# Filler matmuls dealt out anew, and a sum of 17 shared between two engines, in a fused attention and feed-forward kernel

## The chip, the cores and the metric

The kernel runs on one core of one Trainium2 chip. A core has TensorE (matmul; PE in the profile, with its weight loads in a row of their own, PEld), VectorE (DVE), ScalarE (ACT), GpSimd (POOL) and SyncE (SP, which here issues DMAs). Each engine works through its own queue in order, and waits on semaphores for others. TensorE writes to PSUM, eight banks of 512 float32 per partition; GpSimd doesn't reach PSUM. The metric is the time of one execution on the device in microseconds (us); lower is better.

## What is computed

The reference, cut to what matters (S = 2048 rows, D = 512, 32 heads of 16, F = 1792):

```python
def _A_ref(x, wqkv, wo):
    qkv = (x @ wqkv).reshape(B, S, 3, H, Dh).transpose(2, 0, 3, 1, 4)
    q, k, v = qkv[0], qkv[1], qkv[2]
    phi = lambda t: jnp.where(t > 0, t + 1, jnp.exp(t)) + 1e-6
    pq, pk = phi(q), phi(k)
    kv = jnp.einsum("bhsd,bhse->bhde", pk, v)
    z = jnp.einsum("bhsd->bhd", pk)
    num = jnp.einsum("bhqd,bhde->bhqe", pq, kv)
    den = jnp.einsum("bhqd,bhd->bhq", pq, z)[..., None] + 1e-6
    o = num / den
    return o.transpose(0, 2, 1, 3).reshape(B, S, D) @ wo

def _B_ref(x, w_gate, w_up, w_down):
    g = _silu(x @ w_gate)
    u = x @ w_up
    return (g * u) @ w_down

xn = _layernorm(x, axis=-1)
return x + _A_ref(xn, A_wqkv, A_wo) + _B_ref(xn, B_w_gate, B_w_up, B_w_down)
```

The change touches `den`: for each row and head, the sum of 16 products `pq * z` and of 1e-6.

## The kernel before

The 2048 rows are 16 tiles of 128. The kernel goes through four parts, and within each the Python code writes out the order of every engine's queue by calling small helpers; `K.add` records an operation with what it reads and writes, and the semaphore waits follow from that.

1. Up to about 48 us: layernorm, projections of keys and queries, the map phi, and the sums over all rows (key-value and z).
2. To about 68 us: gate and up projections for the first 384 rows (tiles 0 to 2), while weights are rescaled.
3. To about 153 us: gate and up for the other 1664 rows, in fourteen **steps**, one for each 128 columns of F (`for fc in range(NFC)`, L1135). Here a 2 x 2 block product is done with seven block products in place of eight (Strassen and Winograd's scheme). In each step every product is a pair of matmuls of 416 columns (`prod`, L869 to 884), for each of two groups of rows, q = 0 and 1: 28 matmuls.
4. To the end: the down projection of those rows by the same scheme with 256-column matmuls (`dprod`, L1079), six pairs of tiles, with the attention output of each tile added on top (`attn`, L1093, four matmuls). The seam between parts 3 and 4 is called **the passage** here: the end of step 13, `first(0)` (product 1 of the first pair of tiles), what fillers are left, and the first products behind them.

**A step's order.** TensorE: product 1 for q = 0, 1; product 5 for both; then products 2 and 6 of q = 0 and of q = 1; then filler units; then products 3 and 7 of q = 0 and of q = 1; filler units again; then product 4 of both. Between these, for each q:

- ScalarE copies product 1 negated into a second bank (`seed`, L891) and product 5 into SBUF (`keep5`, L896), and takes the silu of two finished banks (`gate0`, L906, and `gate1`, L911).
- VectorE takes the saved product 5 less the bank after product 6 and puts it where product 3 then accumulates (`u4`, L916): product 3 waits for it. After product 7 it saves a difference to `c22` (`up22`, L921), and only then may product 4 accumulate on that bank. After product 4 it multiplies with the silu (`h21`, L931).
- GpSimd multiplies `c22` with the silu (`h22`, L925).

**Beside this a step carries** for VectorE the sums of weight blocks for the next pair of steps (`w_sums`, L842: one operation in even steps, two in odd ones); for ScalarE a rescaling of weights (L834) and, in some steps, a sum of squares over a block of w_down (`square_d`, L782, not needed before step 6's end); and the division by `den` for one tile:

- GpSimd multiplies `pq` with z into `pz` (`pz_mul`, L657), two tiles ahead. `pz` has two buffers of 32 heads by 17 float32: 16 products, and the last place holds 1e-6, written once by ScalarE (`pz_floor`, L650).
- VectorE sums the 17 (`den_sum`, L663) at the end of the step before, and takes the reciprocal (`den_turn`, L669) in the step, between `u4` and `up22`.
- GpSimd multiplies `pq` with it (`pq_mul`, L676), at the end of the step's queue and made to wait for `w_sums`; then comes `pz_mul` of the tile two ahead. SyncE transposes the tile by DMA (`turn`, L682).

Steps 0 to 10 do this for tiles 0 to 10 (their slot numbers are the same); the other five tiles are done in part 4.

**Filler units.** `todo` (L935) holds 72 single matmuls of 512 columns, the down projection and attention of tiles 0 to 3 (`ounits`, L700 to 711: 18 units for each, into banks 0 and 1). `fill(n)` (L938) puts the next n of them on TensorE's queue. Three are put into step 0 at L1140; `FILLS` (L1133) has for each step how many go ahead of product 3 (L1163) and how many between product 7 and product 4 (L1170); what is left goes behind `first(0)` in the passage (L1222). With the 32nd and the 36th unit the results of tiles 0 and 1 are complete, and `oout` adds x on VectorE (L720) and stores the tile; then the banks are used for tiles 2 and 3.

**In the passage** ScalarE copies the last hidden block, rescaled, into the layout of part 4 (`hcopy`, L1061), then copies product 1 (`dseed`, L1101), for which the attention matmuls (L1095) on that bank wait. VectorE then forms sums of hidden blocks (`h_sum`, L1073) and of w_down blocks (`t_sum`, L1024; `t1_part`, L1015), saves one result (`dkeep_y`, L1109) and combines two banks (`du4`, L1115), for which product 7 waits.

Of the kernel before, what the change touches and what calls it, by code (L numbers as in the profile page):

```python
# [7 lines left out]
ALU = mybir.AluOpType  # L8
# [112 lines left out]
def bass_parallel_sum__linear_attn_block__swiglu_ffn__prompt_kernel(nc, A_x, A_wqkv, A_wo, B_x, B_w_gate, B_w_up, B_w_down, out):  # L121
    xin = A_x[0]
    oview = out[0]
    K = _Program()
    bf, f32 = dt.bfloat16, dt.float32

    with contextlib.ExitStack() as es:
        E = es.enter_context

        def sb(name, shape, dtype):  # L130
            return E(nc.sbuf_tensor(name, shape, dtype))
# [17 lines left out]
        pq = sb("pq", [P, NT, D], bf)  # L149
# [9 lines left out]
        zbc = sb("zbc", [P, D], f32)  # L159
        pz = sb("pz", [P, 2, NH * (DH + 1)], f32)  # L160
        den = sb("den", [P, 2, NH], f32)
# [45 lines left out]
        junks = [b_[:, :, :].rearrange("p a b -> p (a b)").bitcast(bf)[:, 0:F // 2] for b_ in (p5, c22)]  # L207
        xs = sb("xs", [P, 2, 2 * H7], f16)
        asd = sb("asd", [P, 8], f32)
# [61 lines left out]
        for t in range(4, 16):  # L271
# [5 lines left out]
            out=ident[:, :], in_=ident[:, :], compare_op=ALU.not_equal, fill=1.0,  # L277
# [362 lines left out]
        def heads(ap):  # L640
            return ap.rearrange("p (h d) -> p h d", d=DH)


        pzh = [pz[:, i, :].rearrange("p (h d) -> p h d", d=DH + 1) for i in (0, 1)]

        def pz_floor(t):
            i = SLOT[t] % 2
            last = pzh[i][:, :, DH:DH + 1].rearrange("p h d -> p (h d)")
            one = nc.const_aps.tensor(1.0, (P, NH), bf)
            K.add("act", lambda e: e.activation(last, one, ACT.Copy, scale=flo[:, t:t + 1] if t in CENTRED else 1e-6),  # L650
                  r=[("flo", t)] if t in CENTRED else [("den", i)], w=[("pz", i)])

        def pz_mul(t, after=()):
            if SLOT[t] < 4:
                pz_floor(t)
            i = SLOT[t] % 2
            K.add("pool", lambda e: e.tensor_tensor(  # L657
                out=pzh[i][:, :, 0:DH], in0=heads(pq[:, t, :]), in1=heads(zbc[:, :]), op=ALU.mult),
                  r=[("pq", t), ("zbc",)] + list(after), w=[("pz", i)])

        def den_sum(t):
            i = SLOT[t] % 2
            K.add("dve", lambda e: e.tensor_reduce(  # L663
                out=den[:, i, :], in_=pzh[i], axis=mybir.AxisListType.X, op=ALU.add),
                r=[("pz", i)], w=[("den", i)])

        def den_turn(t):
# [18 lines left out]
        def divide(t):  # L686
            den_sum(t)
            den_turn(t)
            pq_mul(t)
            turn(t)  # L690
            pz_mul(t + 2)
# [232 lines left out]
        def h22(q, fc):  # L924
            K.add("pool", lambda e: e.tensor_tensor(  # L925
                out=hj(fc)[:, TB + q * TS:TB + (q + 1) * TS], in0=c22[:, q, :], in1=sil4[:, 2 + q, :], op=ALU.mult),
                r=[("c22", q), ("sil4", 2 + q)], w=[("hj", fc, 2 + q)], a=hjold(fc))
# [10 lines left out]
        def fill(n):  # L938
            for _ in range(min(n, len(todo))):
                fn, r, w, after = todo.pop(0)  # L940
                K.add("pe", fn, r=r, w=w)
                busy[w[0]] = after is None
                if after is not None:
                    after()

        for t in (0, 2):
# [15 lines left out]
            "u": top_square, "g": gather, "T": lambda: total(1), "C": lambda: scales(1),  # L962
            "a": lambda k, p: scale(("wg", "wu")[k], p), "p": lambda k, p: scale(("wg", "wu")[k], p, "pool"),
            "X": x_sum, "W": lambda h: w_sums(0, h), "Z": z_total, "z": lambda i: pz_mul(ORDER[i]), "d": square_d,
            "G": lambda c, e: gt_evac(c, "act" if e else "dve"), "m": m_mm, "k": kv_mask,
            "h": gather_d, "D": total_d, "e": scales_d, "s": lambda i: smalls_d()[i]()}

        def prepare(text):
            for w in text.split():
                steps2[w[0]](*[int(v) for v in w[1:]])  # L970
# [7 lines left out]
        for j in range(NFC):  # L978
# [5 lines left out]
            prepare(BESIDE.get(j, ""))  # L984
        Wt = [w_[:, 2 * i:2 * i + 2, 0:2 * H7] for w_ in (wg, wu) for i in (0, 1)]
        wtk = [(key + "c", fc) for key in ("wg", "wu") for fc in range(7)]
# [4 lines left out]
        def split(ap):  # L991
            return ap.rearrange("p (s c) -> p s c", s=2)

        Tt = {2: Wt[0].bitcast(f16), 3: xs[:, :, :], 1: split(mixb[:, 0:4 * H7].bitcast(f16)),
              4: wg[:, 0:2, 2 * H7:].bitcast(f16)}

# [129 lines left out]
        def pz_ahead(t, after=()):  # L1126
            i = SLOT[t] + 2
            if i < NT:
                pz_mul(ORDER[i], after)

        SC = {1: [("wg", 2, "act")], 2: [("wu", 3, "act")], 3: [("wg", 3, "act")], 4: [("wu", 4, "act")], 5: [("wg", 4, "act")], 6: [("wu", 5, "act")], 7: [("wg", 5, "act")], 8: [("wg", 6, "act")], 9: [("wu", 6, "act")]}
        LATE = {10: [(11, 0)], 11: [(11, 1)]}
        FILLS = ((3, 4), (2, 3), (1, 3), (3, 5), (1, 4), (1, 2), (0, 2), (2, 2), (1, 3), (1, 3), (1, 3), (1, 2), (3, 3), (6, 1))  # L1133
        DIV = {i + 0: ORDER[i] for i in range(11)}
        for fc in range(NFC):  # L1135
            for q in (0, 1):
# [15 lines left out]
            p = fc // 2  # L1152
            if fc == 0 and 0 in DIV:
                den_sum(DIV[0])
# [7 lines left out]
            prepare(BESIDE.get(14 + 2 * fc, ""))  # L1162
            fill(FILLS[fc][0])  # L1163
            for q in (0, 1):
# [4 lines left out]
                h22(q, fc)  # L1169
            fill(FILLS[fc][1])  # L1170
            for q in (0, 1):
# [29 lines left out]
            if fc + 1 in DIV:  # L1201
                den_sum(DIV[fc + 1])
# [21 lines left out]
        for p in range(NP2 - 1):  # L1224
            a, b, d = GB[p % 2]
            t = DIV2.get(p)
# [60 lines left out]
        p = NP2 - 1  # L1287
# [58 lines left out]
```

## Time and profile before

| | |
|---|---|
| median of three runs | 200.21 us (200.05 to 200.54) |
| the profiled execution | 200.1 us |
| its span, first to last instruction | 198.9 us |
| granted TensorE clock over the span | 1.00 |
| HBM read, written | 9.70 MB, 2.10 MB |

A row of the profile gives the line of the kernel, the engine, the operation, what it writes and reads by the program's tensor names, the shapes, and how often (x). Times of a timeline row are the start in us from the span's beginning and the duration; in brackets stands how long the engine had been idle and which engine, tensor and line ended that. Neighbouring rows of one kind are merged (x2), and the duration then covers both. In the view of busy time by stretch, each row has the stretch, its length, and the busy time and instruction count of each engine. `pb` is PSUM. `h22` and others write into tensors that served earlier purposes (`hT`, `xn`, `pq`), so one line can show several names. The clock of TensorE was granted in full throughout, so a matmul of a kind takes the same time everywhere.

### The profile page before, as it was taken

Reading aid. Unit: us, or ns where it says so; the run is one execution under the profiler, and the core shown is the slowest. Engines: PE = TensorE matmul, PEld = TensorE weight load, DVE = VectorE, ACT = ScalarE, POOL = GpSimd, SP = SyncE. Lnnn points to the kernel's source line nnn. Section 1 sums busy time; section 2 is a strip of 40 time slices with the busy share of each in tenths; the row PEclk is TensorE's granted clock in tenths of the full one; section 3 lists DMA queues with packets and bytes.
Section 4 is the critical chain, followed back from the end, with each engine's and each line's share of the span. In section 5 each row is a group of like instructions: output and inputs, shape, how many; then the busy total and the mean of one; then the engine's idle time right before and its main releaser. Section 6 shows DMA issues by size and latency. Waiting matters only on the chain.

```text
span 198.9 us, 3554 instructions
## 1 busy us (share of the span) xinstructions
PE 194.7 (98%) x1193; PEld 114.5 (58%) x1207; DVE 172.1 (87%) x328; ACT 157.2 (79%) x314; POOL 124.0 (62%) x152
## 2 busy tenths in 40 slices
PE   8999999999999999999999999999999999999995
PEld 2344444444655545555554455555555788888884
DVE  3999999996997898886899998887987999998886
ACT  4799887699798997998988888998897968575300
POOL 3787877799999388667577667868678004413220
PEclk9999999999999999999999999999999999999999
DMA  6943457899900000111110211111000012132123
GB/s 173 357 130 81 58 107 218 229 289 373 313 4 0 3 0 0 28 30 26 28 40 13 56 26 26 26 26 31 2 0 2 3 40 66 30 79 66 44 67 120
DMA packets 28899, 15.97 MB, mean 80 GB/s; under 512 B 17232, under 2 KB 28880, under 8 KB 28880
## 3 DMA queue, kind: packets, MB, share of 16 engines
q1 hardware_dynamic: 28320, 15.28, 28.8%
q10 hardware_dynamic: 560, 0.46, 0.7%
q8 instruction: 9, 0.15, 0.3%
q14 instruction: 10, 0.08, 0.2%
HBM read 9.70 MB, written 2.10 MB: 59 GB/s over the span
## 4 chain that ended last, share of the span: by engine, by line
PE 94%; DVE 2%; DMA 1%; issue 1%; ACT 0%; POOL 0%; SPq 0%
PE pb L881 35%; PE pb L1089 16%; PE pb L443 13%; PE pb L564 9%; PE pb L492 7%; PE pb L704 5%; PE pb L1095 5%; PE pb L708 2%; DMA x_sb<-in_A_x_dram 1%; PE pb L624 0%; PE pb L696 0%; DVE pq L482 0%; PE pb L406 0%; POOL ef L471 0%; DVE stats L306 0%
## 5 line engine op out<-in xcount | busy, mean ns | idle before, releaser
L676 POOL TENSOR_TENSOR pq<-pq,rden 128x512 bf16<-128x512 bf16 x16 | 16.9, 1056 | 37.2 <-DVE rden L669 26.7
L881 PE MATMUL pb<-xnT,wgu 128*128 128x416 bf16 x112 | 26.6, 339 | 0.0
L443 PE MATMUL pb<-wqkv,xnT 128*128 128x512 bf16 x110 | 25.1, 380 | 0.2
L657 POOL TENSOR_TENSOR pz<-pq,zbc 128x512 f32<-128x512 bf16 x16 | 18.9, 1179 | 5.0 <-ACT pz L650 3.5
L911 ACT ACTIVATE zacc<-pb,iw 128x416 bf16<-128x416 f32 x28 | 16.6, 613 | 4.4 <-PE pb L881 3.5
L564 PE MATMUL pb<-xnT,wgu 128*128 128x384 bf16 x112 | 19.9, 326 | 0.1
L921 DVE TENSOR_TENSOR c<-pb,p 128x416 f32<-128x416 f32 x28 | 16.4, 589 | 3.9 <-PE pb L881 1.9
L925 POOL TENSOR_TENSOR hT<-c,zacc 128x416 bf16<-128x416 f32 x16 | 15.3, 976 | 6.7 <-DVE c L921 4.1
L471 POOL TENSOR_SCALAR ef<-ef 128x512 bf16<-128x512 bf16 x25 | 15.5, 620 | 5.8 <-ACT ef L464 5.6
L443 PEld LDWEIGHTS pb<-wqkv,xnT 128*128 128x128 bf16 x112 | 10.9, 98 | 13.4 <-DVE pk L482 0.4
L916 DVE TENSOR_TENSOR pb<-p,pb 128x416 f32<-128x416 f32 x28 | 16.3, 593 | 2.1 <-PE pb L881 0.8
L464 ACT ACTIVATE ef<-pb 128x512 bf16<-128x512 f32 x25 | 14.8, 593 | 3.9 <-PE pb L443 3.9
L509 POOL TENSOR_TENSOR zacc<-zacc,pk 128x512 f32<-128x512 f32 x13 | 16.0, 1232 | 1.0
L891 ACT ACTIVATE pb<-pb 128x416 f32<-128x416 f32 x28 | 13.4, 500 | 3.4 <-PE pb L881 2.4
L881 PEld LDWEIGHTS pb<-xnT,wgu 128*128 128x128 bf16 x112 | 10.9, 98 | 8.8 <-ACT pb L891 0.3
L906 ACT ACTIVATE zacc<-pb,iw 128x416 bf16<-128x416 f32 x28 | 15.7, 625 | 0.0
L564 PEld LDWEIGHTS pb<-xnT,wgu 128*128 128x128 bf16 x112 | 10.9, 98 | 7.0
L1089 PE MATMUL pb<-wgu,xnT 128*128 128x256 f16 (+1 forms) x112 | 14.9, 273 | 0.0
L881 PE MATMUL pb<-xnT,wqkv 128*128 128x416 bf16 x56 | 14.4, 340 | 0.2
L881 PE MATMUL pb<-GT,wqkv 128*128 128x416 f16 x56 | 14.4, 339 | 0.0
L881 PE MATMUL pb<-wo,wqkv 128*128 128x416 f16 x56 | 14.4, 339 | 0.0
L1095 PE MATMUL pb<-M,pk 128*128 128x256 bf16 x96 | 13.6, 273 | 0.0
(201 smaller groups left out, 489.3 us busy)
## 6 DMA issues: line engine op xcount, KB each, us to landing
x_sb<-in_A_x_dram SPq DMA_DIRECT2D x14, 128.0 KB, 4.1
wgu<-in_B_w_gate_dram SPq DMA_DIRECT2D x2, 896.0 KB, 5.5
wgu<-in_B_w_up_dram SPq DMA_DIRECT2D x2, 896.0 KB, 7.8
wd<-in_B_w_down_dram SPq DMA_DIRECT2D x2, 896.0 KB, 12.4
out_dram<-out_sb SPq DMA_DIRECT2D x24, 64.0 KB, 1.6
wqkv<-in_A_wqkv_dram SPq DMA_DIRECT2D x3, 256.0 KB, 4.7
wqkv<-in_A_wqkv_dram SPq DMA_DIRECT2D x1, 512.0 KB, 6.6
wo<-in_A_wo_dram SPq DMA_DIRECT2D x1, 512.0 KB, 8.3
```

Of the source, the lines that this page charges most:

```text
L443: K.add("pe", [(lambda e, c=c: e.matmul(banks[b][:, :], src[:, c, t * P:(t + 1) * P], wqkv[:, c, col:col + D], start=(c == 0), stop=(c == ...
L509: K.add("pool", lambda e: e.tensor_tensor(out=dst, in0=acc, in1=more, op=ALU.add), r=[key, mkey], w=[dkey])
L564: fns.append(lambda e, c=c, b=b, w_=w_: e.matmul(banks[b][:, 0:T0], w_[:, c, fc * P:(fc + 1) * P], xnT[:, c, 0:T0], start=(c == 0), stop=( ...
L657: K.add("pool", lambda e: e.tensor_tensor(out=pzh[i][:, :, 0:DH], in0=heads(pq[:, t, :]), in1=heads(zbc[:, :]), op=ALU.mult), r=[("pq", t) ...
L676: K.add("pool", lambda e: e.tensor_tensor(out=heads(pq[:, t, :]), in0=heads(pq[:, t, :]), in1=rden[:, i, :][:, :, None].broadcast_to([P, N ...
L881: K.add("pe", [(lambda e, c=c: e.matmul(banks[bank][:, 0:TS], L[i][:, c, :], R[i][:, c, ts], start=(start and c == 0), stop=(c == 1), skip ...
L906: K.add("act", lambda e: e.activation(sil4[:, q, :], bk(a), ACT.Silu, scale=iw[:, 0:1]), r=[B(a), ("iw",)], w=[("sil4", q)], a=[("zacc", 0 ...
L911: K.add("act", lambda e: e.activation(sil4[:, 2 + q, :], bk(d), ACT.Silu, scale=iw[:, 0:1]), r=[B(d), ("iw",)], w=[("sil4", 2 + q)], a=[(" ...
L916: K.add("dve", lambda e: e.tensor_tensor(out=bk(d), in0=p5[:, q, :], in1=bk(b), op=ALU.subtract), r=[B(b), ("p5", q)], w=[B(d)])
L921: K.add("dve", lambda e: e.tensor_tensor(out=c22[:, q, :], in0=bk(b), in1=p5[:, q, :], op=ALU.subtract), r=[B(b), ("p5", q)], w=[("c22", q)])
L1089: K.add("pe", [(lambda e, k=k: e.matmul(split(banks[b][:, 0:HD]), L[:, k, :], cut[:, :, k * P:(k + 1) * P], start=(start and k == 0), stop ...
L1095: K.add("pe", [(lambda e, g=g: e.matmul(dk(b), pk[:, SLOT[t], g * P:(g + 1) * P], M[:, g, lo:lo + HD], start=False, stop=(g == NG - 1), sk ...
```

## The change

It has two parts. `FILLS` gets other counts: in (ahead of product 3, ahead of product 4),

| step | 0 | 1 | 2 | 3 | 4 | 5 | 6 | 7 | 8 to 10 | 11 | 12 | 13 | passage |
|---|---|---|---|---|---|---|---|---|---|---|---|---|---|
| before | 3, 4 | 2, 3 | 1, 3 | 3, 5 | 1, 4 | 1, 2 | 0, 2 | 2, 2 | 1, 3 | 1, 2 | 3, 3 | 6, 1 | 3 |
| after | 3, 4 | 2, 3 | 1, 3 | 3, 3 | 1, 3 | 1, 3 | 1, 3 | 1, 3 | 1, 3 | 1, 2 | 2, 3 | 4, 2 | 5 |

Units keep their order. The 32nd falls in step 4 before and in step 5 after, the 36th in step 6 in both.

And `pz` is laid out anew: 8 products, 1e-6, 8 products for each head. `pz_mul` writes the two halves to their places, for all 16 tiles. For slots 3 to 8 GpSimd then adds the second half to the first (`fold`, 32 x 8 float32, in place), behind `pz_mul` on its queue, so in steps 1 to 6 of the program's order; and VectorE's sum of these six tiles, at the end of steps 2 to 7, reads 9 places per head in place of 17. On the other engines the instructions and their order stay, but for where the units stand and that `oout` of tile 0 moves with its unit.

```diff
+FOLD = range(3, 9)
...
+        def two(ap):
+            return ap.rearrange("p (h c d) -> p h c d", h=NH, c=2)
+
+        def halves(i):
+            v = pz[:, i, :]
+            return bass.AP(v.tensor, v.offset, [list(v.ap[0]), [DH + 1, NH], [DH // 2 + 1, 2], [1, DH // 2]])
+
         pzh = [pz[:, i, :].rearrange("p (h d) -> p h d", d=DH + 1) for i in (0, 1)]
 
         def pz_floor(t):
             i = SLOT[t] % 2
-            last = pzh[i][:, :, DH:DH + 1].rearrange("p h d -> p (h d)")
+            last = pzh[i][:, :, DH // 2:DH // 2 + 1].rearrange("p h d -> p (h d)")
...
             K.add("pool", lambda e: e.tensor_tensor(
-                out=pzh[i][:, :, 0:DH], in0=heads(pq[:, t, :]), in1=heads(zbc[:, :]), op=ALU.mult),
+                out=halves(i), in0=two(pq[:, t, :]), in1=two(zbc[:, :]), op=ALU.mult),
                   r=[("pq", t), ("zbc",)] + list(after), w=[("pz", i)])
+            if SLOT[t] in FOLD:
+                fold(t)
+
+        def fold(t):
+            i = SLOT[t] % 2
+            lo, hi = pzh[i][:, :, 0:DH // 2], pzh[i][:, :, DH // 2 + 1:]
+            K.add("pool", lambda e: e.tensor_tensor(out=lo, in0=lo, in1=hi, op=ALU.add), r=[("pz", i)], w=[("pz", i)])
 
         def den_sum(t):
             i = SLOT[t] % 2
             K.add("dve", lambda e: e.tensor_reduce(
-                out=den[:, i, :], in_=pzh[i], axis=mybir.AxisListType.X, op=ALU.add),
+                out=den[:, i, :], in_=pzh[i][:, :, 0:DH // 2 + 1] if SLOT[t] in FOLD else pzh[i], axis=mybir.AxisListType.X, op=ALU.add),
                 r=[("pz", i)], w=[("den", i)])
...
-        FILLS = ((3, 4), (2, 3), (1, 3), (3, 5), (1, 4), (1, 2), (0, 2), (2, 2), (1, 3), (1, 3), (1, 3), (1, 2), (3, 3), (6, 1))
+        FILLS = ((3, 4), (2, 3), (1, 3), (3, 3), (1, 3), (1, 3), (1, 3), (1, 3), (1, 3), (1, 3), (1, 3), (1, 2), (2, 3), (4, 2))
```

## The prediction

> **What bounds the kernel now.** First the page: the busy shares, and the chain that ended last by engine.
>
> ```profile
> PE 194.7 (98%) x1193; PEld 114.5 (58%) x1207; DVE 172.1 (87%) x328; ACT 157.2 (79%) x314; POOL 124.0 (62%) x152
> PE 94%; DVE 2%; DMA 1%; issue 1%; ACT 0%; POOL 0%; SPq 0%
> ```
>
> TensorE carries the chain from end to end, and the change keeps every one of its matmuls. So the time can fall only by what TensorE still waits, and rise only by new waits. How much it waits is read from the steps. In the view of busy time by stretch I cut steps 3 to 8 where each step's first matmul of product 1 starts. The columns are the stretch, its length, then the busy time of PE, weight loads, VectorE, ScalarE and GpSimd, then clock and DMA.
>
> ```profile
> 87.28:93.93 6.65, 6.65 (x38) 3.52 (x36) 5.01 (x10) 6.08 (x12) 4.83 (x6) 1.00 0.11 22
> 93.93:99.93 6.00, 5.95 (x33) 3.17 (x33) 5.41 (x11) 6.00 (x13) 3.54 (x5) 1.00 0.11 23
> 99.93:105.58 5.65, 5.65 (x33) 2.86 (x31) 5.18 (x11) 5.09 (x10) 4.06 (x5) 1.00 0.18 46
> 105.58:111.17 5.59, 5.54 (x30) 2.69 (x30) 5.30 (x11) 4.98 (x10) 4.09 (x5) 1.00 0.12 23
> 111.17:117.06 5.89, 5.89 (x34) 3.02 (x33) 5.46 (x15) 5.08 (x10) 4.09 (x5) 1.00 0.19 47
> 117.06:122.85 5.79, 5.74 (x33) 3.07 (x33) 5.03 (x11) 5.31 (x12) 4.23 (x5) 1.00 0.11 23
> ```
>
> Steps 3 to 8 hold 8, 5, 3, 2, 4 and 4 filler units. From 6.65 and 6.00 a unit costs (6.65 - 6.00) / 3 = 0.217 us, and the 28 matmuls of a step alone 4.92 (0.176 each); with 4 units that makes 5.79, which step 8 shows. Against 4.92 + 0.217 n, step 5 (5.57) loses 0.08, step 6 (5.35) 0.24, step 7 (5.79, and 0.03 for one small matmul) 0.07: 0.39 us. PE's busy column hides this, since the ends of matmuls are modelled. The weight loads show it, with what they waited for in brackets; step 6, then the passage:
>
> ```profile
> 107.87 0.27 PEld L881 LDWEIGHTS pb<-GT,wqkv 128*128 128x128 f16 x2
> 108.54 0.11 PEld L881 LDWEIGHTS pb<-xnT,wqkv 128*128 128x128 f16 x2 [0.40 <-DVE pb L916]
> ```
> ```profile
> 152.65 0.11 PEld L881 LDWEIGHTS pb<-wqkv,wgu 128*128 128x128 bf16 x2 [0.53 <-DVE c L921]
> ...
> 154.45 0.33 PEld L1095 LDWEIGHTS pb<-M,pk 128*128 128x128 bf16 x4 [0.36 <-ACT pb L1101]
> ...
> 158.57 0.66 PEld L1089 LDWEIGHTS pb<-xs,zacc 128*128 128x128 f16 x7 [0.29 <-DVE pb L1115]
> ```
>
> Not all of a load's idle time is lost. It holds the usual gap between loads and the load's lead over its own matmul, together about one matmul and the gap: 0.25 between 416-column matmuls (0.176 + 0.08, the gap left by 0.27 for two loads of 0.10), 0.33 behind a filler (0.217 + 0.12), 0.12 between the passage's 256-column ones (0.11 + 0.01). So of 0.40 in step 6 about 0.15 is lost, of 0.53 0.28, of 0.36 0.03 and of 0.29 0.17. So product 4 of step 13 loses 0.28 to VectorE's L921, the attention block 0.03, product 7 of the passage 0.17: 0.48. With the steps 0.87 us are within reach.
>
> **Why VectorE is late in steps 5 to 7.** Its queue from the end of step 5 into step 7:
>
> ```profile
> 105.35 1.09 DVE L931 TENSOR_TENSOR hT<-pb,zacc 128x416 bf16<-128x416 f32 x2 [0.19 <-PE pb L881]
> 106.36 0.42 DVE L842 TENSOR_TENSOR wqkv<-wqkv,wgu 128x512 f16<-128x512 f16 x1
> 106.81 0.42 DVE L842 TENSOR_TENSOR wqkv<-wgu,wqkv 128x512 f16<-128x512 bf16 x1
> 107.15 0.71 DVE L663 TENSOR_REDUCE den<-pz 128x32 f32<-128x544 f32 x1
> 107.89 1.30 DVE L916 TENSOR_TENSOR pb<-p,pb 128x416 f32<-128x416 f32 x2
> 109.10 0.34 DVE L669 RECIPROCAL rden<-den 128x32 f32<-128x32 f32 x1
> 109.46 1.29 DVE L921 TENSOR_TENSOR c<-pb,p 128x416 f32<-128x416 f32 x2
> 110.67 0.68 DVE L720 TENSOR_TENSOR out_sb<-pb,x_sb 128x512 bf16<-128x512 f32 x1
> 111.27 1.08 DVE L931 TENSOR_TENSOR hT<-pb,zacc 128x416 bf16<-128x416 f32 x2
> 112.26 0.68 DVE L842 TENSOR_TENSOR wqkv<-wgu 128x1024 f16<-128x1024 bf16 x1
> 112.86 0.15 DVE L787 TENSOR_REDUCE as<-asd 128x1 f32<-128x8 f32 x1
> 113.05 0.16 DVE L790 TENSOR_SCALAR as1b<-as 128x1 bf16<-128x1 f32 x1
> 113.12 0.71 DVE L663 TENSOR_REDUCE den<-pz 128x32 f32<-128x544 f32 x1
> 113.75 1.08 DVE L916 TENSOR_TENSOR pb<-p,pb 128x416 f32<-128x416 f32 x2
> ```
>
> From L916 to L916 it needs 5.86, in a step that TensorE could do in 5.35. Two things load it: the output row L720 (in steps 4 and 6, where units 32 and 36 end) and a step made short by few fillers.
>
> **The fillers.** Steps 3 to 7 now hold 6, 4, 4, 4 and 4 units, 22 as before, so TensorE's own work in them stays 29.4. Unit 32 and its L720 move to step 5; unit 36 stays in step 6. What does VectorE need in a step of 5.79? Take t = 0 at L916, which starts 2.31 into step 6: ten matmuls (1.76) and 0.55 for a pair to run through. Product 4's first pair is then done at 24 x 0.176 + 4 x 0.217 + 0.55 = 5.64, t = 3.33. There L931 starts; L842 is done at 5.0 in even steps and 5.2 in odd ones, den (0.71) at 5.64 and 5.83, and the next L916 is due at 5.79. L720 fits the gap between L921 (done by 2.95) and L931 and pushes that by only 0.11; the two small operations of step 6 add 0.34. Fillers alone would leave L916 late by some 0.15 in step 6 and 0.25 in step 7.
>
> **The shorter sum** takes that away. den reads 288 values in place of 544. From L663 (0.71 for 544) and L787 (0.15 for 8) a value costs 1.05 ns, so 0.44: 0.27 less, six times (0.34 less if it halved; nothing if its 32 rows set the price). At 0.44 den is done at 5.67 in step 5 and 5.77 in step 6, in time for 5.79. The 0.39 goes, unless ScalarE is late.
>
> **ScalarE, which the new deal uncovers.** In the table steps 3 and 4 keep it busy 6.08 + 6.00 = 12.08 us; they shrink from 12.65 to 6.22 + 5.79 = 12.01.
>
> ```profile
> 93.54 0.94 ACT L782 ACTIVATE xs<-wd 128x896 bf16<-128x896 bf16 x1
> 94.38 0.19 ACT L782 ACTIVATION_READ_ACCUMULATOR xs<-wd 128x1 f32 x1
> 94.48 0.98 ACT L891 ACTIVATE pb<-pb 128x416 f32<-128x416 f32 x2
> 95.37 0.92 ACT L896 ACTIVATE p<-pb 128x416 f32<-128x416 f32 x2
> ```
>
> L782 is a sum of squares with no reader nearby, but L891 and L896 stand behind it, and L916 waits for the first L896, done at about 95.89 (a pair takes 0.92 with some overlap). Two units fewer bring step 4 to 93.50, its L916 due at 93.50 + 2.31 = 95.81; L896 holds it to 95.92. The single filler ahead of product 3 hides L916 almost exactly, so step 4 loses 0.1 (0 to 0.25). Step 5 has ScalarE busy for 5.09 only and recovers. Net for steps 3 to 7: 0.39 - 0.10 = 0.29.
>
> **Steps 12, 13 and the passage.** One unit leaves each step and both go behind product 1 of the passage, so TensorE comes to step 13's products 3 and 4 one and up to two units (0.43) earlier, and has five units to fill the passage.
>
> ```profile
> 151.30 1.29 DVE L921 TENSOR_TENSOR c<-pb,p 128x416 f32<-128x416 f32 x2 [0.59 <-PE pb L881]
> 152.57 1.24 DVE L931 TENSOR_TENSOR pq<-pb,zacc 128x416 bf16<-128x416 f32 x2
> 154.16 0.63 DVE L1073 TENSOR_TENSOR xn<-wqkv,xn 128x896 f16<-128x896 bf16 x1 [0.36 <-ACT xn L1061]
> ```
>
> L921 idles 0.59 for product 7, so it can come 0.59 earlier, while product 4 comes 0.43 earlier: its wait falls from 0.28 to 0.12. L916 of step 13 has less cover; I put 0.06 on that. The attention block's 0.03 goes. That is 0.28 - 0.12 - 0.06 + 0.03 = 0.13. Then L931, ScalarE's copy L1061 and L1073 follow in a chain that starts at product 4's first pair, 0.43 - 0.06 = 0.37 earlier. VectorE has no idle from L1073 to near L1115, so that comes 0.37 earlier, TensorE 0.13: product 7's 0.17 goes too. Sum 0.30 (0.10 to 0.45).
>
> **What GpSimd pays.**
>
> ```profile
> 110.13 1.91 POOL L925 TENSOR_TENSOR hT<-c,zacc 128x416 bf16<-128x416 f32 x2 [0.64 <-DVE c L921]
> 113.02 1.06 POOL L676 TENSOR_TENSOR pq<-pq,rden 128x512 bf16<-128x512 bf16 x1 [0.98 <-DVE as L787]
> 114.04 1.16 POOL L657 TENSOR_TENSOR pz<-pq,zbc 128x512 f32<-128x512 bf16 x1
> ```
>
> No row has the fold (256 values, float32). From L657 (512 in 1.16) and L925 (416 in 0.96) a value costs 2.1 ns and an instruction 0.09: 0.63, and some 0.08 to wait for the product it adds. Its bounds are 0.58 (half of L657) and 0.96 (L925). Behind it on the queue stands L925, which idles 0.64 there: it comes 0.1 later, and only the next step's L921 waits for its buffer. L657 now writes runs of 8 for all 16 tiles: between 1.06 (L676) and twice its price, 2.3; I take 1.16, as the runs of 16 that it writes now cost 2.3 ns a value, what L925's whole rows cost. The Trainium skill speaks against the fold: "GPSIMD Engine Reference", section 4.1, gives elementwise work to VectorE because GpSimd is about 2x slower at it. By that rule 0.63 buys 0.27 here, which matters only if GpSimd is on the path (rival b); the page has it 62% busy.
>
> **Sum.** 0.29 + 0.30 = 0.59, less 0.03 for a den later than I count it: 0.56. The profiled run took 200.1 (a span of 198.9 and 1.2 around it) and the median of three runs is 200.21: 199.54 on the one, 199.65 on the other. I forecast 199.6.
>
> **Rivals.**
> (a) *The waits only change place*: 200.1. For it: one filler hides L916 with almost nothing to spare in every step, ScalarE is late in step 4, den may cost by rows. Steps 3 to 7 then gain 0.1 and the passage 0.05. Against it: step 8 waits for nothing with the same 4 units and a den of 0.71.
> (b) *GpSimd becomes the loop, slower than before*. L676 waits for L842; L657, the fold and two L925 follow it; and L842 is held up when it meets L925:
>
> ```profile
> 147.14 1.38 DVE L1024 TENSOR_TENSOR wgu<-wgu,mixb 128x896 f16<-128x896 bf16 x1
> ```
>
> An operation of this size took 0.63 with GpSimd idle (L1073 above); here 1.38, beside L925. The loop is 0.08 + 2.18 for L676 and L657 + 0.71 + 1.91 + 0.55 to 0.85 for L842: 5.4 to 5.7, against 5.79. It decides once L657 and the fold take over 2.0 together and not 1.8. At 2.3 + 0.63 it is 0.9 over in each of six steps, 5.6 us in all; a tenth of that excess already eats the gain. A middling case, 2.3 together (1.4 and 0.9): 0.3 x 6 - 0.56 = 1.2 slower, 201.4; at 2.17, 200.7. The Trainium skill, "SBUF — State Buffer", section "Who interferes with whom", has it that a VectorE operation with two SBUF inputs and a GpSimd one that reads SBUF block each other entirely; the 1.38 agrees.
> (c) *All 0.87 goes*, step 4's wait too: 199.3.
>
> **Chances.** Forecast 0.48, (a) 0.25, (b) 0.15, (c) 0.12. About 0.3% (0.6 us) is what a measurement of this kernel can tell from no change. The forecast's 0.56 lies next to that line: of its 0.48 I give 0.24 to faster and 0.24 to within. Faster: 0.24 + 0.12 + 0.02 of (a) = 0.38. Slower: 0.15 + 0.03 of (a), should step 4 lose its whole 0.25 and more = 0.18. Within: 0.44. The range is 199.2 to 200.8, from just past (c) to the milder half of (b); the forecast's own, by its bounds, 199.3 to 200.0.
>
> **What would show it.** Right: steps 4 to 7 at 5.79 to 5.9 each, no load idle of 0.40 at product 3 of step 6, den at 0.44, a fold of about 0.63 done before VectorE's first L921 ends, no wait at product 7 of the passage; in step 4 L916 starting with ScalarE's L896. Wrong: L657 over 1.3, L842 stretched beside L925 in steps 2 to 7, steps over 5.9, or a den that stays near 0.7.

## The result, and the profile after

| | before | after |
|---|---|---|
| median | 200.24 us (13 runs, 200.05 to 201.43) | 199.59 us (13 runs, 199.34 to 200.25) |
| span of the profiled execution | 198.9 us | 198.3 us |

The ratio is 0.9959, with a 95% interval of 0.9945 to 0.9972: about 0.4% faster. In the changed kernel line numbers are higher, by 15 behind the fold: u4 is L931 (L916 before), up22 L936 (L921), h21 L946 (L931), h22 L940 (L925), seed L906 (L891), keep5 L911 (L896), pz_mul L665, the fold L674, den_sum L678, pq_mul L691, w_sums L857, the sum of squares L797, a step's matmuls L896. The page after, busy shares and chain:

```profile
PE 194.6 (98%) x1193; PEld 115.8 (58%) x1207; DVE 171.1 (86%) x328; ACT 157.2 (79%) x314; POOL 128.3 (65%) x158
PE 97%; DVE 1%; issue 0%; POOL 0%; ACT 0%
```

TensorE still carries the chain, with 97% in place of 94%; VectorE's 2% are 1% now. Where the time went is seen in the view of busy time by stretch, cut where each part's first weight load starts: steps 0 to 2, 3 to 7, 8 to 12, and step 13 to the end. Before, then after:

```profile
68.12:87.10 18.98, 18.88 (x102) 9.92 (x103) 16.57 (x29) 17.37 (x37) 13.91 (x13) 1.00 0.07 14
87.10:116.89 29.79, 29.69 (x163) 15.26 (x164) 26.32 (x54) 27.24 (x51) 20.62 (x21) 1.00 0.14 32
116.89:146.11 29.22, 29.06 (x159) 15.42 (x161) 24.63 (x46) 26.27 (x53) 21.86 (x22) 1.00 0.09 19
146.11:198.86 52.75, 50.46 (x429) 41.12 (x428) 46.23 (x88) 29.55 (x43) 14.83 (x15) 1.00 0.18 49
```
```profile
68.29:87.28 18.99, 18.89 (x103) 9.94 (x104) 16.56 (x29) 17.38 (x37) 14.60 (x14) 1.00 0.07 14
87.28:116.80 29.52, 29.41 (x162) 15.66 (x163) 25.37 (x53) 27.21 (x51) 23.95 (x27) 1.00 0.14 32
116.80:145.81 29.01, 28.85 (x158) 15.34 (x160) 24.40 (x46) 26.22 (x53) 21.56 (x22) 1.00 0.09 19
145.81:198.33 52.52, 50.36 (x430) 41.45 (x429) 46.15 (x88) 29.60 (x43) 15.40 (x15) 1.00 0.19 49
```

The first column is the one to read. Steps 3 to 7 give 0.26 (the ends of the stretches are rounded), step 8 to the end 0.21 + 0.23 = 0.44 (of the 0.21, almost all is one filler that moved behind step 13). From step 0 on that is 130.74 - 130.04 = 0.70. The part before step 0, in which only the places of `pz` that are written differ, ends at 68.12 in the one profile and at 68.29 in the other, and takes back 0.17. Such shifts come with every profile (68.12 to 68.75 over all those of this study), so below kernels are compared from step 0 on. There, a part without a change repeats to within 0.03.

The steps 3 to 8 after:

```profile
87.45:93.67 6.22, 6.22 (x36) 3.32 (x34) 4.75 (x10) 5.65 (x11) 5.08 (x7) 1.00 0.12 24
93.67:99.59 5.92, 5.87 (x32) 2.99 (x32) 4.83 (x11) 5.92 (x14) 4.21 (x5) 1.00 0.11 24
99.59:105.38 5.79, 5.79 (x34) 3.07 (x33) 5.37 (x11) 5.51 (x10) 5.08 (x7) 1.00 0.11 23
105.38:111.16 5.78, 5.73 (x32) 3.07 (x32) 5.33 (x13) 5.06 (x10) 4.69 (x6) 1.00 0.18 45
111.16:116.98 5.82, 5.82 (x35) 3.22 (x34) 5.10 (x15) 5.08 (x10) 4.90 (x6) 1.00 0.20 48
116.98:122.77 5.79, 5.74 (x33) 3.08 (x33) 4.84 (x11) 5.24 (x12) 4.13 (x5) 1.00 0.11 23
```

Steps 5, 6 and 7 take what TensorE's own work takes (5.79, and 0.03 more in step 7); step 4 loses 0.13. The weight loads of step 4 (product 2 of q = 0) and of the passage:

```profile
95.20 0.11 PEld L896 LDWEIGHTS pb<-xnT,wgu 128*128 128x128 bf16 x2 [0.37 <-ACT pb L906]
```
```profile
151.91 0.11 PEld L896 LDWEIGHTS pb<-wqkv,wgu 128*128 128x128 bf16 x2 [0.31 <-DVE c L936]
...
153.93 0.51 PEld L1110 LDWEIGHTS pb<-M,pk 128*128 128x128 bf16 x4
...
158.06 0.66 PEld L1104 LDWEIGHTS pb<-xs,zacc 128*128 128x128 f16 x7
```

Product 4 of step 13 waits less (0.31 idle against 0.53, and the load ahead of it doesn't wait any more), the attention matmuls and product 7 not at all. The view of waits adds up what the steps' loads waited for up22. Before, then after:

```profile
PEld pb L881 <- DVE c L921: 2.0, 6, 0.5
```
```profile
PEld pb L896 <- DVE c L936: 0.6, 2, 0.3
```

Six waits became two. And the two new prices, from the groups by shape:

```profile
L678 DVE TENSOR_REDUCE den<-pz 128x32 f32<-128x544 f32 x10 | 7.1, 709 | 0.0
L678 DVE TENSOR_REDUCE den<-pz 128x32 f32<-128x288 f32 x6 | 2.7, 444 | 0.0
L674 POOL TENSOR_TENSOR pz<-pz 128x256 f32<-128x256 f32 x6 | 4.0, 671 | 0.5
L665 POOL TENSOR_TENSOR pz<-pq,zbc 128x512 f32<-128x512 bf16 x16 | 18.9, 1180 | 5.0 <-ACT pz L658 3.5 <-DVE xn L1088 1.5
```

### The profile page after: what moved, and what is told of

Same layout as the page of the kernel before. It is cut to its first block, busy times and chain, and to the rows that moved or that the text cites. A ratio compares the mean times of both kernels' runs of the same rounds, so it can differ in the third digit from the quotient of the medians.

```text
span 198.3 us, 3560 instructions
## 1 busy us (share of the span) xinstructions
PE 194.6 (98%) x1193; PEld 115.8 (58%) x1207; DVE 171.1 (86%) x328; ACT 157.2 (79%) x314; POOL 128.3 (65%) x158
## 4 chain that ended last, share of the span: by engine, by line
PE 97%; DVE 1%; issue 0%; POOL 0%; ACT 0%
PE pb L896 35%; PE pb L1104 16%; PE pb L444 13%; PE pb L565 9%; PE pb L493 7%; PE pb L719 6%; PE pb L1110 5%; PE pb L297 2%; PE pb L723 2%; PE pb L407 1%; PE pb L625 0%; PE pb L711 0%; DVE pq L483 0%; POOL ef L472 0%; ACT ef L465 0%
## 5 line engine op out<-in xcount | busy, mean ns | idle before, releaser
L691 POOL TENSOR_TENSOR pq<-pq,rden 128x512 bf16<-128x512 bf16 x16 | 16.9, 1056 | 36.6 <-DVE rden L684 26.9
L896 PE MATMUL pb<-xnT,wgu 128*128 128x416 bf16 x112 | 26.6, 339 | 0.0
L665 POOL TENSOR_TENSOR pz<-pq,zbc 128x512 f32<-128x512 bf16 x16 | 18.9, 1180 | 5.0 <-ACT pz L658 3.5
L931 DVE TENSOR_TENSOR pb<-p,pb 128x416 f32<-128x416 f32 x28 | 16.4, 594 | 3.4 <-PE pb L896 1.7
L936 DVE TENSOR_TENSOR c<-pb,p 128x416 f32<-128x416 f32 x28 | 16.4, 588 | 3.2 <-PE pb L896 1.1
L940 POOL TENSOR_TENSOR hT<-c,zacc 128x416 bf16<-128x416 f32 x16 | 15.3, 975 | 2.8 <-ACT zacc L926 1.5
L906 ACT ACTIVATE pb<-pb 128x416 f32<-128x416 f32 x28 | 13.5, 502 | 3.3 <-PE pb L896 2.3
L896 PEld LDWEIGHTS pb<-xnT,wgu 128*128 128x128 bf16 x112 | 10.9, 98 | 8.9 <-ACT pb L906 0.4
L921 ACT ACTIVATE zacc<-pb,iw 128x416 bf16<-128x416 f32 x28 | 15.7, 628 | 0.0
L896 PE MATMUL pb<-xnT,wqkv 128*128 128x416 bf16 x56 | 14.4, 339 | 0.3
L896 PE MATMUL pb<-wo,wqkv 128*128 128x416 f16 x56 | 14.4, 339 | 0.0
L896 PE MATMUL pb<-GT,wqkv 128*128 128x416 f16 x56 | 14.4, 339 | 0.0
L307 DVE BATCH_NORM_STATS2 stats<-x_sb 128x6 f32<-128x512 bf16 x16 | 10.8, 678 | 3.2 <-DMA x_sb<-in_A_x_dram 3.1
```

The lines of the kernel that those rows point to most:

```text
L665: K.add("pool", lambda e: e.tensor_tensor(out=halves(i), in0=two(pq[:, t, :]), in1=two(zbc[:, :]), op=ALU.mult), r=[("pq", t), ("zbc",)] + ...
L691: K.add("pool", lambda e: e.tensor_tensor(out=heads(pq[:, t, :]), in0=heads(pq[:, t, :]), in1=rden[:, i, :][:, :, None].broadcast_to([P, N ...
L896: K.add("pe", [(lambda e, c=c: e.matmul(banks[bank][:, 0:TS], L[i][:, c, :], R[i][:, c, ts], start=(start and c == 0), stop=(c == 1), skip ...
L921: K.add("act", lambda e: e.activation(sil4[:, q, :], bk(a), ACT.Silu, scale=iw[:, 0:1]), r=[B(a), ("iw",)], w=[("sil4", q)], a=[("zacc", 0 ...
L931: K.add("dve", lambda e: e.tensor_tensor(out=bk(d), in0=p5[:, q, :], in1=bk(b), op=ALU.subtract), r=[B(b), ("p5", q)], w=[B(d)])
L936: K.add("dve", lambda e: e.tensor_tensor(out=c22[:, q, :], in0=bk(b), in1=p5[:, q, :], op=ALU.subtract), r=[B(b), ("p5", q)], w=[("c22", q)])
```

## The experiments

The ratio is to the kernel before, measured on the same chip (its median lay between 200.24 and 200.34, so the ratios compare better than the medians); the other columns are from one profile of each, cut like the four parts above (us, from each kernel's own step 0).

| kernel | median | ratio (95%) | steps 0-2 | 3-7 | 8-12 | 13 to end | from step 0 |
|---|---|---|---|---|---|---|---|
| before | 200.24 | 1 | 18.98 | 29.78 | 29.22 | 52.75 | 130.74 |
| after | 199.59 | 0.9959 (0.9945 to 0.9972) | 18.99 | 29.53 | 29.01 | 52.52 | 130.04 |
| fillers only | 199.59 | 0.9964 (0.9951 to 0.9977) | 18.99 | 29.56 | 29.01 | 52.53 | 130.09 |
| fold only | 200.30 | 0.9997 (0.9987 to 1.0007) | 18.99 | 29.78 | 29.23 | 52.75 | 130.75 |
| passage only | 199.84 | 0.9982 (0.9972 to 0.9992) | 18.99 | 29.78 | 29.01 | 52.54 | 130.31 |
| steps and fold | 200.15 | 0.9992 (0.9982 to 1.0002) | 18.99 | 29.53 | 29.22 | 52.74 | 130.48 |
| second add on GpSimd | 200.94 | 1.0027 (1.0017 to 1.0037) | 18.99 | 30.59 | 29.31 | 52.53 | 131.43 |
| square early | 199.50 | 0.9963 (0.9943 to 0.9982) | 18.99 | 29.39 | 29.01 | 52.53 | 129.92 |
| fold for all 16 | 200.39 | 0.9999 (0.9991 to 1.0008) | 19.39 | 29.53 | 29.33 | 52.54 | 130.79 |
| square early, filler to step 11 | 199.90 | 0.9979 (0.9965 to 0.9992) | 18.99 | 29.17 | 29.57 | 52.53 | 130.27 |
| square early, no fold | 199.62 | 0.9958 (0.9934 to 0.9981) | 18.99 | 29.42 | 29.01 | 52.53 | 129.95 |
| the same with late scaling | 199.37 | 0.9952 (0.9928 to 0.9975) | 18.99 | 29.17 | 29.15 | 52.52 | 129.84 |
| and step 0 dealt anew | 199.27 | 0.9939 (0.9918 to 0.9959) | 18.86 | 29.17 | 29.15 | 52.52 | 129.70 |

("The same with late scaling" builds on the row "square early, filler to step 11".)

**The fillers without the fold.**

```diff
-FOLD = range(3, 9)
+FOLD = ()
```

> The changed kernel with GpSimd's fold taken out: the new deal of the fillers stays, and VectorE sums all 17 values of each head (den 0.71 us, 544 values) in steps 3 to 8 again. Theory of the prediction: den is then 0.27 us longer in every step, L931 (the add that opens product 3) comes about 0.15 late in step 6 and 0.25 in step 7, and since a late L931 is handed from step to step, steps 5 to 7 together lose 0.2 to 0.4: 199.8 to 200.0 us against 199.6 for the changed kernel; the trace shows product 3's load of steps 6 and 7 idle for 0.35 or more. Rival: VectorE is in time without the fold, since step 8 waits for nothing with a den of 0.71: 199.6, and steps 5 to 7 at 5.79 each.

The rival won: 199.59 like the changed kernel, 0.05 more from step 0 on. VectorE's u4 in steps 6 and 7, in the changed kernel and in this one:

```profile
107.69 1.30 DVE L931 TENSOR_TENSOR pb<-p,pb 128x416 f32<-128x416 f32 x2
...
113.47 1.30 DVE L931 TENSOR_TENSOR pb<-p,pb 128x416 f32<-128x416 f32 x2
```
```profile
106.97 0.71 DVE L678 TENSOR_REDUCE den<-pz 128x32 f32<-128x544 f32 x1
107.60 1.24 DVE L931 TENSOR_TENSOR pb<-p,pb 128x416 f32<-128x416 f32 x2
...
112.82 0.71 DVE L678 TENSOR_REDUCE den<-pz 128x32 f32<-128x544 f32 x1
113.45 1.18 DVE L931 TENSOR_TENSOR pb<-p,pb 128x416 f32<-128x416 f32 x2
```

Counted from the steps' first weight loads (105.20 and 110.99 in the one, 105.05 and 110.84 in the other), u4 starts at 2.49 and 2.48 with the fold, at 2.55 and 2.61 without: 0.06 and 0.13 late, where the theory had 0.15 and 0.25. And lateness is not handed on: the pair takes 1.30 when its second half waits for TensorE, but 1.24 and 1.18 when it is late, so the second half is on time again. Step 6 still takes 5.79 and step 7 5.85 in place of 5.81.

**The fold with the fillers of before.**

```diff
-        FILLS = ((3, 4), (2, 3), (1, 3), (3, 3), (1, 3), (1, 3), (1, 3), (1, 3), (1, 3), (1, 3), (1, 3), (1, 2), (2, 3), (4, 2))
+        FILLS = ((3, 4), (2, 3), (1, 3), (3, 5), (1, 4), (1, 2), (0, 2), (2, 2), (1, 3), (1, 3), (1, 3), (1, 2), (3, 3), (6, 1))
```

> The changed kernel with the fillers of the kernel before: the fold alone. Theory of the prediction: a step with few fillers ahead of product 3 loses its time whatever VectorE has to sum, since the wait is for the add that follows product 6 of the same step; so step 6 (no filler there) keeps most of its 0.24, and only the queue's lateness in step 7 (0.07) and a little of steps 5 and 6 goes; the passage keeps its 0.48. 200.1 us, 0.1 less than the kernel before. Rival 1: the fold by itself frees the steps: 199.9 or less, with steps 5 to 7 at 5.57, 5.35 and 5.79. Rival 2, GpSimd as the loop: the short step 6 (5.35) is less than the loop of 5.4 to 5.7, so the fold makes step 6 or 7 longer than now: 200.3 or more.

Not even the 0.1: nothing. Its steps 5 to 7:

```profile
99.94:105.59 5.65, 5.65 (x33) 2.88 (x32) 5.01 (x11) 5.10 (x10) 4.55 (x6) 1.00 0.18 46
105.59:111.18 5.59, 5.59 (x31) 2.69 (x30) 5.12 (x11) 4.99 (x10) 4.70 (x6) 1.00 0.12 23
111.18:117.07 5.89, 5.89 (x35) 3.06 (x33) 5.30 (x15) 5.08 (x10) 4.93 (x6) 1.00 0.19 47
```

They are those of the kernel before, 5.65, 5.59 and 5.89, to the hundredth, though VectorE works 0.16 to 0.18 less in each. So VectorE's queue did not set them. What does is the deal itself. With three fillers between product 7 and product 4 no step of the two kernels loses anything there. With two, as in steps 5, 6, 7 and 11, a step loses 0.07, and with one, as in step 13 before, 0.07 + 0.217 = 0.28: the fillers cover the time from product 7 over up22 to product 4's load, and each one that is missing shows. Likewise one filler ahead of product 3 just covers u4, and step 6, with none, loses 0.17 there, which makes its 0.24 with the 0.07.

**The two halves of the deal, each alone.** The kernel before with the new counts of steps 12 and 13, and the changed kernel with the old ones:

```diff
-(3, 3), (6, 1))
+(2, 3), (4, 2))
```

> The kernel before with one change: the fillers of steps 12 and 13 as in the changed kernel, (2,3) and (4,2), so that two more stand behind product 1 of the passage. Steps 3 to 7 and GpSimd stay as before. Theory of the prediction: product 4 of step 13 waits 0.12 or less, product 7 of the passage not at all: 0.30 less than before by the prediction's sum, 0.43 by what the changed kernel's trace shows from step 8 to the passage; 199.8 to 199.95 us. If VectorE's t_sum (L1024 here) comes ahead of GpSimd's second L925 again, it takes 0.7 in place of 1.4, and the 0.43 holds. Rival: that gain needed the fold (the deal of steps 3 to 7 or GpSimd's moved times): 200.1 to 200.2.

```diff
-(2, 3), (4, 2))
+(3, 3), (6, 1))
```

> The changed kernel with the fillers of steps 12 and 13 as before, (3,3) and (6,1): the new deal of steps 3 to 7 and the fold stay. Theory of the prediction: the gain of steps 3 to 7 alone, 0.25 to 0.29: 199.95 to 200.0 us, with steps 5 to 7 at 5.79 and 0.1 lost in step 4, and product 4 of step 13 and product 7 of the passage waiting for 0.28 and 0.17 as before. The two parts add up: this one's gain and that of the passage alone together make the 0.6 to 0.7 of the whole. Rival: the steps' gain is given back at the passage, where VectorE is late whatever came before: 200.1 to 200.2.

From step 0 on they gain 0.43 and 0.26, and 0.69 together against 0.70 for the whole: the parts add up and neither needs the other. The times (0.9982 and 0.9992) agree with that, but are too blunt to show it. In the passage, product 4's wait falls from 0.28 to 0.07, by the rule of two fillers in place of one.

**A second add on GpSimd behind each fold**, whose result nothing reads:

```diff
             K.add("pool", lambda e: e.tensor_tensor(out=lo, in0=lo, in1=hi, op=ALU.add), r=[("pz", i)], w=[("pz", i)])
+            K.add("pool", lambda e: e.tensor_tensor(out=hi, in0=lo, in1=hi, op=ALU.add), r=[("pz", i)], w=[("pz", i)])
```

> The changed kernel with a second add of the fold's size on GpSimd behind each of the six folds (it writes the upper halves, which nothing reads afterwards): GpSimd gets 0.67 us and some 0.08 of waiting more in each of the six tiles. Theory of the prediction's rival (b), GpSimd as the loop from L691 over L665, the folds, two L940 and L857 back to L691: the loop grows from 5.4 to 5.7 to 6.15 to 6.45, against steps of 5.79, so each of steps 3 to 8 loses 0.35 to 0.65: 201.5 to 203.5 us, and L940 comes so late that it delays the next step's L936. The other theory, from the idle 0.6 to 1.0 ahead of each L691 in the changed kernel's trace: that idle takes it up, den is 0.75 later (L678 waits for the second add) and L931 late by part of that: 0 to 0.3 in each step, 199.6 to 201.0.

The result, 200.94, lies below the one theory's range and inside the other's, but by the trace both have a part. Steps 3 to 5 lose nothing: GpSimd's idle takes the 0.75 up. Steps 6, 7 and 8 lose 0.45, 0.60 and 0.30. In step 7 (lines of this kernel are one higher: L941 is h22, L858 w_sums):

```profile
111.61 1.91 POOL L941 TENSOR_TENSOR hT<-c,zacc 128x416 bf16<-128x416 f32 x2
114.14 1.06 POOL L692 TENSOR_TENSOR pq<-pq,rden 128x512 bf16<-128x512 bf16 x1 [0.63 <-DVE as L803]
```
```profile
112.55 1.51 DVE L858 TENSOR_TENSOR wqkv<-wgu 128x1024 f16<-128x1024 bf16 x1
```

h22 now ends at 113.52, after w_sums wants to start, and holds it up: 1.51 in place of 0.68. den and u4 come late behind it, and TensorE pays. In the changed kernel the h22 of that step ends at 112.07 and w_sums starts at 112.12:

```profile
110.16 1.91 POOL L940 TENSOR_TENSOR hT<-c,zacc 128x416 bf16<-128x416 f32 x2
```
```profile
112.12 0.68 DVE L857 TENSOR_TENSOR wqkv<-wgu 128x1024 f16<-128x1024 bf16 x1
```

So in that step the fold had brought h22 to within 0.05 us of w_sums; in the run of the fillers without the fold the gap is 0.2.

**The fold for all 16 tiles.**

```diff
-FOLD = range(3, 9)
+FOLD = range(0, 16)
```

> The changed kernel with the fold for all 16 tiles in place of six. Theory: no wait of TensorE in steps 0 to 2, 9, 10 and the passage ends with den, so VectorE's 0.27 less per tile buys nothing there and GpSimd's 0.67 more costs nothing as long as its loop stays under 5.79: 199.5 to 199.7. Rival: in steps 9 and 10 or the passage GpSimd is late with its products (there it also copies for the passage), and the time rises by 0.2 or more.

The rival's sign was right, not its place: steps 0 and 12 lose 0.40 and 0.32, the passage nothing. In step 0 a fold lands on VectorE's product of 128 x 1664, here and, for the same product, in the changed kernel:

```profile
69.09 0.66 POOL L674 TENSOR_TENSOR pz<-pz 128x256 f32<-128x256 f32 x1
```
```profile
69.21 1.42 DVE L857 TENSOR_TENSOR GT<-xnT,ef 128x1664 f16<-128x1664 bf16 x1
```
```profile
69.19 1.01 DVE L857 TENSOR_TENSOR GT<-xnT,ef 128x1664 f16<-128x1664 bf16 x1
```

In step 12 a fold ahead of h22 makes h22 later. The second operation of w_sums takes 1.08 in place of 0.42, and u4 behind it starts 0.47 later in the step than in the changed kernel. No run tried this reading by itself.

**One sum of squares earlier.** It moves from the end of step 3 to the middle of step 1 ("d0" in the table of what goes beside each product: from place 21 to place 16):

```diff
-13: "X2 a12 z1 p11 p01 X4", 14: "d6 d3", 18: "d4", 21: "d0", 22: "d2",
+13: "X2 a12 z1 p11 p01 X4", 14: "d6 d3", 16: "d0", 18: "d4", 22: "d2",
```

> The changed kernel with one sum of squares on ScalarE (L797, 1.13 us with its read) moved from the end of step 3 to the middle of step 1. Theory: in step 4 product 2 waits for the seed's read of its bank (L906), which stands behind that L797 and a scale (L849); with it gone ScalarE is in time, step 4 takes 5.79 in place of 5.92, and the kernel is 0.13 faster: 199.46. Rival: the sum of squares is late wherever it stands, since ScalarE is full from step 1 to step 4 too: step 1 or 2 loses the 0.13 in its place, 199.6.

Step 4 takes 5.79 and all from step 0 on 129.92, 0.12 less than the changed kernel: as expected in the trace, below what the times can tell. The order of ScalarE in the changed kernel's step 4, which starts at 93.49, shows the cause: a scaling and the sum of squares, and the seed only behind them at 94.64. In this run it starts 0.73 into the step, which would have been 94.22.

```profile
92.67 1.14 ACT L849 ACTIVATE wgu<-wgu,sw 128x1024 bf16<-128x1024 bf16 x1
93.71 0.94 ACT L797 ACTIVATE xs<-wd 128x896 bf16<-128x896 bf16 x1
94.55 0.19 ACT L797 ACTIVATION_READ_ACCUMULATOR xs<-wd 128x1 f32 x1
94.64 0.90 ACT L906 ACTIVATE pb<-pb 128x416 f32<-128x416 f32 x2
```

> The changed kernel with the sum of squares moved to step 1 (as in the run before that did this alone) and with no fold at all. By the run of the fillers alone the fold is worth 0.03 to 0.05 us, at step 7 only. Theory: what bounds the steps is the number of fillers behind product 6 and behind product 7, not VectorE's sum; so steps 3 to 7 take 29.39 + 0.03 to 0.05, and all from step 0 on 129.95 to 130.0 (129.92 with the fold): 199.5 us. Rival: with ScalarE in time, VectorE's longer sum becomes the last to come in steps 5 to 7, each loses 0.1 or more: 199.7 or more.

That kernel is the one with the earlier sum of squares and `FOLD = ()`. It takes 129.95 from step 0 on, as the first theory has it: the fold is worth 0.03.

**One more filler for step 11.** With ScalarE relieved, step 3 can give one away:

```diff
-        FILLS = ((3, 4), (2, 3), (1, 3), (3, 3), (1, 3), (1, 3), (1, 3), (1, 3), (1, 3), (1, 3), (1, 3), (1, 2), (2, 3), (4, 2))
+        FILLS = ((3, 4), (2, 3), (1, 3), (2, 3), (1, 3), (1, 3), (1, 3), (1, 3), (1, 3), (1, 3), (1, 3), (1, 3), (2, 3), (4, 2))
```

> The changed kernel with that sum of squares moved to step 1 and one filler moved from step 3 (now 2 and 3) to step 11 (now 1 and 3). Theory: step 4 loses nothing (0.13 gained), and step 11, which loses 0.07 with 3 fillers, runs at 5.79 with 4 and loses nothing, while step 3 has ScalarE time to spare once the sum of squares has gone: 0.20 faster than the changed kernel, 199.4. Rival: step 3 with 5 fillers leaves ScalarE as late at step 4 as it was, so only the 0.07 of step 11 comes: 199.5; or the fillers that now run one step later find their inputs late: 199.6 or more.

It came out slower than the changed kernel, by 0.23 from step 0 on. Steps 3 to 7 and step 11 (5.79) went as expected, and step 12 took 6.42 in place of 6.00, for a reason that neither theory had. GpSimd's scaling of M (L843) and VectorE's block sum (L1030):

```profile
143.31 1.12 POOL L843 TENSOR_SCALAR M<-M,sm 128x1024 bf16<-128x1024 bf16 x1
```
```profile
143.36 1.48 DVE L1030 SCALAR_TENSOR_TENSOR mixb<-wd,sd,wgu 128x384 f16<-128x384 bf16 x1
```

In the changed kernel the two start the other way round:

```profile
143.59 1.51 POOL L843 TENSOR_SCALAR M<-M,sm 128x1024 bf16<-128x1024 bf16 x1
```
```profile
143.50 0.61 DVE L1030 SCALAR_TENSOR_TENSOR mixb<-wd,sd,wgu 128x384 f16<-128x384 bf16 x1
```

Whoever is first, by 0.05 or 0.09, runs at its own pace, and the other takes longer, by 0.87 or 0.39. With step 11 a filler longer, w_sums at the start of step 12 no longer met h22 (0.41 in place of 0.62), and GpSimd's copy and the scaling behind it came 0.13 earlier in the step, ahead of L1030. The first up22 behind L1030 then was done 0.77 later in the step, 0.35 of that was covered, and product 4 came 0.42 late. Whether this reading holds was tried by taking the scaling out of the way, behind GpSimd's copies at the end of step 12:

```diff
-            if fc in [10, 11]:
-                m_scale([10, 11].index(fc))
+            if fc in [10, 12]:
+                m_scale([10, 12].index(fc))
```

> The run that moved the sum of squares and gave step 11 a fourth filler, with one more edit: GpSimd's second scaling of M (L843) is queued behind the copies that end step 12, no longer between the two copies L1018 of step 12. Theory: in that run the scaling started 0.05 ahead of VectorE's L1030 (128x384) and held it for 0.87 (1.48 in place of 0.61), which made L936 and product 4 of step 12 late by 0.42; with the scaling gone from there L1030 takes 0.61 again, steps 8 to 12 take 29.15 in place of 29.57, all from step 0 on 129.85: 199.4 us. Rival 1: L1030 waits for something else, and step 12 keeps its 0.42. Rival 2: the scaling, now late, holds up the passage (it must be done before the attention block reads M) or VectorE's operations of step 13: 0.2 or more lost behind step 13.

Steps 8 to 12 take 29.15, from step 0 on 129.84, and the block sum of step 12 its own time again:

```profile
143.47 0.61 DVE L1030 SCALAR_TENSOR_TENSOR mixb<-wd,sd,wgu 128x384 f16<-128x384 bf16 x1
```

**Step 0 dealt anew**, on top of that:

```diff
-        FILLS = ((3, 4), (2, 3), (1, 3), (2, 3),
+        FILLS = ((4, 3), (2, 3), (1, 3), (2, 3),
```

> The run with the late scaling, and in step 0 four fillers ahead of product 3 and three behind it in place of three and four. Theory: step 0 loses 0.12 because L931 comes late (VectorE's long products L857 stand ahead of it); the fourth filler ahead covers that, and three behind product 7 are enough for product 4, as in steps 1 to 10: steps 0 to 2 take 18.87 to 18.92 in place of 18.99, all from step 0 on 129.75: 199.3 us. Rival: L936 of step 0 is as late as L931, since VectorE's queue sets it, and with three fillers behind product 7 the loss comes back at product 4: no gain.

Steps 0 to 2 take 18.86, and 129.70 from step 0 on: 1.04 less than the kernel before and 0.34 less than the changed one. 199.27 us, 0.9939 of the kernel before (0.9918 to 0.9959), is the fastest of the study; over the changed kernel the gain is shown by the traces, while the intervals of the two ratios overlap.

## Why the prediction was right, and which of its reasons was not

199.6 was forecast and 199.59 measured; the sum of 0.56 stands against 0.70 from step 0 on, and 0.65 between the medians. That the time fits to 0.01 is luck: steps 3 to 7 gave the 0.26 of the sum (0.29 less 0.03), but step 8 to the end gave 0.44 in place of 0.30, and the part before step 0 shifts by more than that difference from profile to profile. Point by point:

- *TensorE carries the chain; a step is 4.92 + 0.217 a filler; 0.39 is lost in steps 5 to 7 and 0.48 at the passage.* Right: steps 5 to 7 no longer lose their 0.39, and the two halves of the deal, run alone, add up.
- *"Why VectorE is late in steps 5 to 7" and "The shorter sum takes that away."* This step failed. The fold alone changed no step, and the fillers alone did all but 0.03 to 0.05. Those losses were the uncovered time behind products 6 and 7, which in these steps depends on the counts alone. The rows show that VectorE was not late in step 6 before: counted from the step's first matmul, as the prediction counts, u4 starts at 107.89 - 105.58 = 2.31 there, and at 107.69 - 105.38 = 2.31 in step 6 after, which loses nothing. In step 7 before it was 0.27 late (113.75 - 111.17 = 2.58), and the two fillers ahead of product 3 covered that. The time held all the same, because the 0.39 was read from the lengths of the steps, and the new counts cover both waits.
- *Fillers alone would leave u4 0.15 and 0.25 late.* Measured 0.06 and 0.13. The sum let u4 start when den is done, but it starts 0.08 before the end of den's row (107.60 against 106.97 + 0.71, 113.45 against 112.82 + 0.71). For step 6 the terms as given, 5.64 + 0.11 + 0.34, make 6.09, and 5.82 with the shorter sum, not the 5.77 that it states. And the sum took lateness for lost time, while the pair of u4 makes up for 0.1 of it.
- *Step 4 loses 0.1 to ScalarE.* The size was right (0.13) and so was the engine, shown by the moved sum of squares. The place was not: product 2 waits for the seed, L906, not product 3 for L931 behind L911. Net for steps 3 to 7, 0.29 forecast, 0.26 measured.
- *Steps 12, 13 and the passage: 0.30.* Measured 0.43. The mechanism held; the term mis-sized is product 4's wait, put at 0.12 and found at 0.07, and the 0.06 put on product 3 of step 13, which lost nothing. The second filler behind product 7 is worth its whole 0.217, and what remained is what every step with two such fillers loses (0.31 idle, here and in steps 5, 6, 7 and 11 before). VectorE's chain then comes 0.43 earlier (counted from step 8), not 0.37, and the waits of the attention block and of product 7 went, as forecast.
- *What GpSimd pays.* The fold took 0.67 (0.63 forecast), the sum 0.44 (0.44), and pz_mul 1.18 as before (1.16): runs of 8 cost it nothing. In step 6 h22 starts only behind the fold (109.53 to 110.20), 0.18 later in the step than without it, where 0.1 was forecast; no step paid for that.
- *Rival (b), GpSimd as the loop.* It did not set in here, but it is real. With 0.75 more for each tile it set in after the first steps and turned the gain of 0.70 from step 0 on into a loss of 0.69, by the way that the rival names: h22 holds up w_sums. Steps 6 to 8 then took 6.24, 6.41 and 6.09, near the 6.15 to 6.45 that had been reckoned for the loop. What that reckoning left out is GpSimd's idle time, which took the longer loop up until then.
- *Rivals (a) and (c).* Steps 3 to 7 gained 0.26, so the waits did not just change place; and 0.13 in step 4 and 0.07 at product 4 of step 13 stayed, so not all of it went.

## What to carry to other kernels

Before speeding up the engine that a wait names, ask whether it is behind with its queue or whether the wait is the bare time of a dependence that too little other work covers: here the count of fillers behind a product settled it, and 0.27 us less of VectorE's work in each of six steps bought 0.03 to 0.05 in all. Such cover is worth most where one unit is missing, and nothing above what covers the wait, so spread it evenly. When operations of VectorE and GpSimd that hold each other up nearly meet, look which starts first: a change upstream by some hundredths can move the end by 0.4.

## What the runs showed of the hardware

Where an operation of VectorE with two inputs in SBUF met one of GpSimd that reads SBUF, the one that started first kept its time, and the second was held for most of what was left of the first (0.87 of 1.07 in the case of L1030): L1030 took 1.48 behind L843 and 0.61 ahead of it, the product of 128 x 1664 took 1.42 beside a fold and 1.01 without, w_sums 1.51 beside h22 and 0.68 without.

The Trainium skill, "SBUF — State Buffer", section "Who interferes with whom", states that the one which issues first keeps the shared ports for its whole instruction. The runs agree on who is held, and the delay they show is 0.1 to 0.2 shorter than that. Up22 (L936), which takes one of its inputs from PSUM, was not held: its pair took 1.29 in step 6 of the changed kernel beside the fold and h22.

The order doesn't always matter. At the end of step 12 VectorE has two such operations in a row, and GpSimd's h22 meets one of them: before it was the first, after the second.

```profile
147.14 1.38 DVE L1024 TENSOR_TENSOR wgu<-wgu,mixb 128x896 f16<-128x896 bf16 x1
148.45 0.74 DVE L1015 SCALAR_TENSOR_TENSOR mixb<-wd,sd,wgu 128x512 f16<-128x512 bf16 x1
```
```profile
146.84 0.67 DVE L1039 TENSOR_TENSOR wgu<-wgu,mixb 128x896 f16<-128x896 bf16 x1
147.44 1.46 DVE L1030 SCALAR_TENSOR_TENSOR mixb<-wd,sd,wgu 128x512 f16<-128x512 bf16 x1
```

The two together take 2.1 either way, so this change of order, striking as it looks in the profile, gave nothing. Even where h22 was done early enough to hold up neither for long (0.73 and 0.74 in the kernel with the late scaling), step 13 to the end takes the same 52.52.

Not tried: the best kernel without the fold, and why the part before step 0 ends at a time that differs by up to 0.6 us between profiles.
